# Experts whose first 128 slots take only batches 0 to 2, in a retention-plus-experts kernel

## The chip, the cores and the metric

The kernel runs on one core of a Trainium2 chip. The engines are named as the profile names them: PE (TensorE, matrix products), DVE (VectorE), ACT (ScalarE), POOL (GpSimd), SP (SyncE); DMA queues are fed by SP, ACT and POOL. The metric is the device time of one execution in microseconds, as the median of several runs. Before the change it is 261.54 us (three runs, 259.69 to 262.08). The profiled execution took 259.74 us, and its trace spans 257.9 us of that; times inside the kernel are counted from the start of that span.

## What is computed

Two stages follow each other. The first is a retention layer (4 batches, 8 heads, 768 tokens, head size 64). Its output rows are the input of the second, a mixture of 8 experts of which each row takes one, or none.

```python
def _attn_ref(q, k, v):                       # state decays by gamma of the head
    for t in range(S):
        state = gamma * state + einsum('bhd,bhe->bhde', k[:, :, t], v[:, :, t])
        y[:, :, t] = scale * einsum('bhd,bhde->bhe', q[:, :, t], state)

def _moe_ref(x, w_skip, w_gate, w1, w2):      # x: 3072 rows of 512
    do_compute = x @ w_skip > 0
    out = x.copy()                            # rows that are skipped stay as they are
    xc = x[do_compute]
    e_idx = argmax(xc @ w_gate)               # 8 experts, one for each row
    gate_w = softmax(xc @ w_gate)[e_idx]
    for e in range(8):
        h = maximum(xc[mask] @ w1[e], 0)      # 512 -> 1024
        y[mask] = gate_w[mask] * (h @ w2[e])  # 1024 -> 512
    out[do_compute] = xc + y
```

In the given input 1510 of the 3072 rows are computed. Counted from the reference's own input, an expert gets 133 to 229 rows of all four batches, and 98 to 164 rows of batches 0 to 2.

## The kernel before

The retention stage goes through 16 units (4 batches, 4 pairs of heads each). A unit's result is spread over two iterations: iteration `i` makes the masked products of unit `i` and adds up unit `i-1`.

```python
    for i in range(NU):                       # NU = 16
        scale_qk(i + 1)                       # POOL: decay factors into k and q
        if i == 0:
            more_constants()                  # POOL iotas, DVE casts
        if i in wunits:
            load_w(*wjobs.pop(0), poolW)      # weights of experts 0 to 3, POOL queue
        load(i + 3)
        for g in range(G):
            t_qk(i, kw, KT, "KT", 1, g)       # PE transposes, ACT copies
            t_qk(i, qw, QT, "QT", 2, g)
        s_at(i, 0)                            # PE products, DVE mask (ATm)
        if i >= 2:
            t_x(i - 2, 0); t_x(i - 2, 1)      # PE transposes to rows, ACT copies, rows to DRAM
        if i >= 1:
            s_inter(i - 1)                    # PE into Y (two PSUM tiles)
        # ... steps of the routing of an earlier batch ...
        s_at(i, 1); s_kv(i); s_av(i - 1, 0); s_at(i, 2); s_av(i - 1, 1)
```

`s_av` ends with two copies out of PSUM that free `Y`:

```python
        xT[i] = pool.tile([128, NS, 128], FP32, tag="xT", bufs=5, name="xT")
        for c in range(2):
            (V_.tensor_copy if c == 1 and i == NU - 1 else A_.copy)(out=xT[i]..., in_=Y[i, c]...)
```

Routing gives each computed row a slot of its expert: 256 slots an expert (`CAP`), in two halves of 128 (`NST = 2`). A row's place is a running count over the rows before it (`places`, `put_places`); one-hot matrices and a matmul (`one_hots`, `slot_table`) turn places into a table `T` of slot to row (`slot_rows` gives the indices `si`) and slot to gate weight (`slot_gates` gives `g`). For batches 0 to 2 this is done inside the loop. For batch 3 it comes after the last unit, in a row:

```python
    L = gate_rows(range(NP - 1))
    s_av(z, 0); s_av(z, 1)
    gate_last(z, L)
    t_x(z, 0); t_x(z, 1)                      # the last rows of `out` leave
    Ls, ha = route(L)
    cp = places(B - 1, ha)
    put_rhs(B - 1, ha, IDS)
    put_places(B - 1, ha, cp)
    oh = one_hots(pool, B - 1)
    slot_table(psum, B - 1, oh, IDS, "T", 4)
    si = slot_rows()
    gate_weight(B - 1, Ls, ha)
    put_rhs(B - 1, ha, GTS)
    slot_table(psum, B - 1, oh, GTS, "T", 4)
    g = slot_gates()
```

Only then come the experts. Rows are fetched from `out` by slot with an indirect DMA, put through the two layers, and written back with an indirect DMA. The weights of experts 4 to 7 are loaded in this stage (`late`: eight loads of 1 MB as bf16), since they take the space of the retention stage.

```python
    for e in range(3):
        gather(e, si, first=True)             # two halves of 128 rows
        load_w(*late.pop(0))
    x_tr(0)                                   # DVE cast, PE transposes, DVE copy
    for e in range(E):
        hT = layer1(e)                        # 32 matmuls, N = 256; ACT relu
        if e + 1 < E:
            x_tr(e + 1)
        layer2(e, hT, si, g, first=True)      # 16 matmuls, N = 512; DVE gate and add; scatter
        with tc.issue_after(scatters[-1].ins):
            if e + 3 < E:
                gather(e + 3, si, first=True)
            for _ in range(2):
                if late:
                    load_w(*late.pop(0))
```

After the experts the kernel reads how many rows the fullest expert has, and repeats the stage for slots above 256 if there are any. Here there are none.

Of the kernel before, what the change touches and what calls it, by code (L numbers as in the profile page):

```python
# [18 lines left out]
def kernel(  # L19
# [24 lines left out]
    R = 3  # L44
# [11 lines left out]
    NEARLY = 4  # L56
    scale = 1.0 / math.sqrt(D)
    lng = [math.log(1.0 - 2.0 ** (-5.0 - h)) for h in range(H)]

    poolC = ctx.enter_context(tc.tile_pool(name="constp", bufs=1))  # L60
    poolW = ctx.enter_context(tc.tile_pool(name="wpool", bufs=1))

# [3 lines left out]
    psum = st1.enter_context(tc.tile_pool(name="rps", bufs=1, space=bass.MemoryType.PSUM))  # L66
    stM = ExitStack()
    ET = mybir.EngineType
    stM.enter_context(tc.manual_schedule(engines={ET.PE, ET.DVE, ET.Activation, ET.Pool, ET.SP}))
# [69 lines left out]
    NV = 6  # L139
# [17 lines left out]
    def clear_table():  # L157
        V_.memset(T[:, :, :, :], 0.0)
        V_.memset(T[:, :, 0, :], float(N // (128 * R)))

    def more_constants():
# [7 lines left out]
        chv_i = poolC.tile([128, NCHT], I32, name="chv_i")  # L169
        G_.iota(chv_i[:, :], pattern=[[1, NCHT // R], [0, R]], base=-(N // (128 * R)), channel_multiplier=0)  # L170
        row_i = poolC.tile([128, 1], I32, name="row_i")
        G_.iota(row_i[:, :], pattern=[[0, 1]], base=0, channel_multiplier=1)
        r_i = poolC.tile([128, NCHT], I32, name="r_i")
        G_.iota(r_i[:, :], pattern=[[0, NCHT // R], [1, R]], base=0, channel_multiplier=0)
# [10 lines left out]
        V_.tensor_copy(vals[:, :, 0], chv_i[:, :])  # L185
        V_.tensor_copy(vals[:, :, 1], row_i[:, :].to_broadcast([128, NCHT]))
        V_.tensor_copy(vals[:, :, 2], r_i[:, :])
# [7 lines left out]
    def load_w(e, which, pl):  # L195
        if which == 0:
            w1b[e] = pl.tile([128, NDB, F], BF16, tag=f"w1_{e}", bufs=1, name="w1b")
            G_.dma_start(out=w1b[e][:, :, :], in_=moe_w1[e].rearrange("(p a) f -> p a f", p=128))
        else:
            w2b[e] = pl.tile([128, NFB, DM], BF16, tag=f"w2_{e}", bufs=1, name="w2b")  # L200
            G_.dma_start(out=w2b[e][:, :, :].rearrange("p (j r) d -> p j (r d)", r=2), in_=moe_w2[e].rearrange("(j p r) d -> p j (r d)", p=128, r=2))
# [73 lines left out]
    def s_av(i, g):  # L275
# [11 lines left out]
        xT[i] = pool.tile([128, NS, 128], FP32, tag="xT", bufs=5, name="xT")  # L287
        for c in range(2):
            (V_.tensor_copy if c == 1 and i == NU - 1 else A_.copy)(  # L289
                out=xT[i][:, :, 64 * c : 64 * c + 64], in_=Y[i, c][:, :, :].rearrange("p g (r t) -> p (g r) t", r=R)  # L290
            )

    def t_x(i, a):
# [5 lines left out]
        if last and a == 0:  # L299
            xall["last"] = pool.tile([128, NS, 128], FP32, tag="xlast", bufs=1, name="xlast")  # L300
# [15 lines left out]
        else:  # L316
            cs = slice(DM - 128, DM) if last else slice(0, DM - 128)
            src = xall["last"][:, :, :] if last else xall[b][:, :, cs]
            for g in range(G):
                A_.dma_start(  # L320
                    out=rows[g * 128 * R : (g + 1) * 128 * R, cs].rearrange("(p r) d -> p r d", r=R),
                    in_=src[:, g * R : (g + 1) * R, :],
                )

# [13 lines left out]
    def gate_rows(pairs, halves=(0, 1), L=None):  # L338

        n = len(pairs)  # L340
        if L is None:
            L = pool.tile([128, NS, E + 1], FP32, tag="L", bufs=2, name="L")
# [17 lines left out]
    def st(name, shape, dt=FP32):  # L360
        return pool.tile(shape, dt, tag=name, bufs=1, name=name)
# [42 lines left out]

    def put_rhs(b, ha, ns):
# [7 lines left out]
    def gate_weight(b, Ls, ha):  # L413
# [4 lines left out]
        rs = st("rs", [128, E])  # L418
        V_.tensor_reduce(out=rs[:, :], in_=ha[:, :, :].rearrange("p c e -> p e c"), axis=AXX, op=ALU.add)  # L419
        V_.tensor_tensor(Rsum[:, :], Rsum[:, :], rs[:, :], ALU.add)  # L420
# [5 lines left out]
        gp = vals[:, js, :]  # L426
        V_.tensor_copy(gp[:, :, 3], gw[:, :])
        V_.tensor_tensor(gw[:, :], gw[:, :], gp[:, :, 3], ALU.subtract)
        V_.tensor_copy(gp[:, :, 4], gw[:, :])
        V_.tensor_tensor(gp[:, :, 5], gw[:, :], gp[:, :, 4], ALU.subtract)  # L430

    def one_hots(pl, b):
        oh = []
        for j in range(b * NS, (b + 1) * NS):
            o = pl.tile([128, CAP], BF16, tag="oh", bufs=NS, name="oh")
            V_.tensor_scalar(o[:, :], iotab[:, :], posT[:, j : j + 1], None, ALU.is_equal)
            oh.append(o)
        return oh

    def slot_table(ps, b, oh, ns, tag, bufs):  # L440

        tp = ps.tile([128, NST, ns.stop - ns.start, E], FP32, tag=tag, bufs=bufs, name="tabps")
        for s_ in range(NST):
# [5 lines left out]
        V_.tensor_tensor(T[:, :, ns, :], T[:, :, ns, :], tp[:, :, :, :], ALU.add)  # L449


    ALLV, IDS, GTS = slice(0, NV), slice(0, 3), slice(3, NV)
    wjobs = [(e, w) for e in range(NEARLY) for w in range(2)]
    wunits = (1, 3, 5, 7, 9, 11, 13, 14)
    routed = oh = None
    for i in range(NU):
        scale_qk(i + 1)
        if i == 0:
# [5 lines left out]
        for g in range(G):  # L464
            t_qk(i, kw, KT, "KT", 1, g)
            t_qk(i, qw, QT, "QT", 2, g)
        s_at(i, 0)
        if i >= 2:
# [4 lines left out]
        if i >= 6 and p == 3:  # L473
            slot_table(psum, b - 1, oh, ALLV, "T", 4)
        if i >= 2 and p == 3:
            gate_logits(b, range(NP))
        if i >= 6 and p == 0:
            L = gate_rows(range(NP))
        if i >= 6 and p == 1:
            cp = places(b - 1, routed[1])  # L480
        s_at(i, 1)
        s_kv(i)
        if i >= 1:
            s_av(i - 1, 0)
        s_at(i, 2)
        if i >= 1:
# [4 lines left out]
        if i >= 6 and p == 0:  # L491
            routed = route(L)
        if i >= 6 and p == 1:
            put_places(b - 1, routed[1], cp)
            oh = one_hots(pool, b - 1)
        if i >= 6 and p == 2:
# [5 lines left out]
    gate_weight(B - 2, *routed)  # L502
    put_rhs(B - 2, routed[1], ALLV)
# [4 lines left out]
    slot_table(psum, B - 2, oh, ALLV, "T", 4)  # L508
    L = gate_rows(range(NP - 1))
    s_av(z, 0)  # L510
# [4 lines left out]
    Ls, ha = route(L)  # L515
    cp = places(B - 1, ha)
    put_rhs(B - 1, ha, IDS)
    put_places(B - 1, ha, cp)
    oh = one_hots(pool, B - 1)
    slot_table(psum, B - 1, oh, IDS, "T", 4)  # L520

    def slot_rows():

        sh = [128, NST, E]
        sf = poolC.tile(sh, FP32, tag="sf", bufs=1, name="sf")
        V_.scalar_tensor_tensor(out=sf[:, :, :], in0=T[:, :, 1, :], scalar=float(R), in1=T[:, :, 2, :], op0=ALU.mult, op1=ALU.add)
        si = poolC.tile(sh, I32, tag="si", bufs=1, name="si")
        V_.scalar_tensor_tensor(
            out=si[:, :, :], in0=T[:, :, 0, :], scalar=float(128 * R), in1=sf[:, :, :], op0=ALU.mult, op1=ALU.add
        )  # L530
        return si

    def slot_gates():
        g = poolC.tile([128, NST, E], FP32, tag="g", bufs=1, name="g")
        V_.tensor_tensor(g[:, :, :], T[:, :, 3, :], T[:, :, 4, :], ALU.add)
        V_.tensor_tensor(g[:, :, :], g[:, :, :], T[:, :, 5, :], ALU.add)
        return g

    si = slot_rows()
    gate_weight(B - 1, Ls, ha)  # L540
    put_rhs(B - 1, ha, GTS)
    slot_table(psum, B - 1, oh, GTS, "T", 4)
    g = slot_gates()
    st1.close()


    poolX = ctx.enter_context(tc.tile_pool(name="wlate", bufs=1, reuse_waits="tile"))
    poolE = ctx.enter_context(tc.tile_pool(name="esb", bufs=2, reuse_waits="tile"))
    psE = ctx.enter_context(tc.tile_pool(name="eps", bufs=2, space=bass.MemoryType.PSUM, reuse_waits="tile"))
# [140 lines left out]
```

## Time and profile before

| Stage | from, us | to, us | what ends it |
|---|---|---|---|
| first loads and constants | 0 | 6.7 | first PE transposes |
| retention, 16 units | 6.7 | 160.1 | last matmul of `s_av(15)` |
| routing of batch 3, first gathers | 160.1 | 173.9 | first matmul of layer 1 |
| eight experts | 173.9 | 245.9 | last matmul of layer 2 |
| last scatters, count, end | 245.9 | 257.9 | end of the span |

PE is busy 215.5 us of the span (84%), DVE 134.2, POOL 95.5, ACT 77.5. The table is read as follows: where PE is busy nearly all the time, its work sets the length of the stage; where it is not, something that PE waits for does. A line `line engine op out<-in` of the profile names the source line, the engine, and the tiles; in the list of waits, `A <- B: t, n, m` says that engine and tile A waited for B for t us in all, n times, the longest m us.

### The profile page before, as it was taken

The numbers are of one execution on the slowest core, as the hardware profiler recorded it, in microseconds if no ns is written. First come the engines' busy times: TensorE is split into PE (matmuls) and PEld (weight loads), VectorE is DVE, ScalarE is ACT, GpSimd is POOL, SyncE is SP. The second block draws the span as 40 slices with busy tenths as digits, with TensorE's granted clock in tenths as the row PEclk, the third lists the DMA queues.
The fourth block names the chain that finished last, engine by engine and source line by source line (L and its number), as shares of the span: only waits on it lengthen the run. The fifth ranks groups of instructions, "written<-read, shape, count | busy, mean of one in ns | idle before, by whom it ended". The sixth has DMA issues, their size and how long they took to land. (4 is left out here: it accounts for less than half of the span.)

```text
span 257.9 us, 7338 instructions
## 1 busy us (share of the span) xinstructions
PE 215.5 (84%) x3121; PEld 169.9 (66%) x3129; DVE 134.2 (52%) x402; ACT 77.5 (30%) x174; POOL 95.5 (37%) x100
## 2 busy tenths in 40 slices
PE   0689999999999999999999988529999395999910
PEld 0468788868987878888778876427666254566600
DVE  3676566635757764766864674672453142334210
ACT  2202553263145335314524513103222303023300
POOL 6635252434244333343423000084475264252230
PEclk9979999999999999999999999756999979799995
DMA  6977949779989499799398604269999999631120
GB/s 200 333 204 187 267 137 206 211 201 230 347 212 243 130 226 315 221 245 260 79 187 256 121 4 158 89 140 220 257 217 220 253 215 269 202 99 59 51 79 0
DMA packets 36788, 48.67 MB, mean 189 GB/s; under 512 B 3236, under 2 KB 29348, under 8 KB 35728
## 3 DMA queue, kind: packets, MB, share of 16 engines
q0 software_dynamic: 7936, 22.97, 42.1%
q1 hardware_dynamic: 26400, 18.90, 24.4%
q10 hardware_dynamic: 2416, 6.29, 6.2%
q8 instruction: 26, 0.43, 0.7%
q14 instruction: 10, 0.08, 0.1%
HBM read 56.64 MB, written 10.49 MB: 260 GB/s over the span
## 5 line engine op out<-in xcount | busy, mean ns | idle before, releaser
L235 DVE TENSOR_TENSOR ATm<-atps,maskc 128x384 f32<-128x384 f32 x96 | 49.0, 552 | 43.4 <-PE atps L230 42.9
L230 PE MATMUL atps<-QT,KT 64*64 64x192 f32 x768 | 44.7, 342 | 6.8 <-ACT QT L217 3.9
L95 POOL TENSOR_TENSOR ks<-kw,tk 128x768 f32<-128x768 f32 x16 | 23.9, 1492 | 44.9 <-PE kvps L251 42.4
L230 PEld LDWEIGHTS atps<-QT,KT 64*64 64x64 f32 x768 | 28.5, 136 | 16.2 <-ACT QT L217 7.5
L281 PE MATMUL yps<-ATm,vn 64*64 64x192 f32 x768 | 38.9, 325 | 0.0
L590 ACT ACTIVATE hT<-hps 128x512 bf16<-128x512 f32 x32 | 19.1, 597 | 59.1 <-PE hps L586 59.1
L95 POOL TENSOR_TENSOR qs<-qw,tq 128x768 f32<-128x768 f32 x15 | 22.7, 1516 | 35.2 <-issue 34.0
L289 ACT COPY xT<-yps 128x384 f32<-128x384 f32 x31 | 13.4, 482 | 71.4 <-PE yps L281 71.4
L586 PE MATMUL hps<-xgT,w1b 128*128 128x256 bf16 x256 | 31.6, 285 | 0.5 <-DVE xgT L578 0.5
L597 PE MATMUL yps<-w2b,hT 128*128 128x512 bf16 x120 | 31.1, 405 | 0.6 <-issue 0.2
L281 PEld LDWEIGHTS yps<-ATm,vn 64*64 64x64 f32 x768 | 30.4, 133 | 0.3 <-issue 0.2
L586 PEld LDWEIGHTS <-w1b 128*128 128x128 bf16 x256 | 26.3, 103 | 6.1 <-issue 0.7
L557 POOL DMA_INDIRECT xg<-out_dram,si x16 | 16.9, 1055 | 34.9 <-DVE rs L419 28.7
L605 POOL DMA_INDIRECT out_dram<-yo,si x16 | 16.6, 1039 | 35.1 <-DVE yo L602 30.1
L602 DVE SCALAR_TENSOR_TENSOR yo<-yps,g,xg 128x512 f32<-128x512 f32 x16 | 12.0, 751 | 23.6 <-PE yps L597 23.6
L597 PEld LDWEIGHTS <-hT 128*128 128x128 bf16 x128 | 13.0, 104 | 15.3 <-issue 3.7
L216 PE MATMUL tps<-ident,ks 128*128 128x128 f32 x96 | 17.3, 291 | 6.7 <-POOL ks L95 6.7
L217 ACT COPY KT<-tps 128x384 f32<-128x384 f32 x32 | 16.1, 505 | 14.2 <-PE tps L216 14.2
L270 PE MATMUL yps<-QT,Zb 128*128 128x192 f32 x96 | 18.5, 328 | 1.0 <-ACT xT L289 1.0
L216 PEld LDWEIGHTS tps<-ident,ks 128*128 128x128 f32 x96 | 11.2, 145 | 11.0 <-POOL ks L95 6.7
L571 DVE CAST xb<-xg 128x512 bf16<-128x512 f32 x16 | 9.6, 638 | 16.1 <-DMA xg<-out_dram,si 16.0
L217 ACT COPY QT<-tps 128x384 f32<-128x384 f32 x32 | 16.5, 516 | 0.5 <-PE tps L216 0.5
(107 smaller groups left out, 241.5 us busy)
## 6 DMA issues: line engine op xcount, KB each, us to landing
w1b<-in_moe_w_dram POOLq DMA_DIRECT2D x8, 1024.0 KB, 11.6
w2b<-in_moe_w_dram POOLq DMA_DIRECT2D x8, 1024.0 KB, 10.4
kw<-in_k_dram SPq DMA_DIRECT2D x16, 384.0 KB, 5.7
qw<-in_q_dram SPq DMA_DIRECT2D x16, 384.0 KB, 4.8
vn<-in_v_dram SPq DMA_DIRECT2D x16, 384.0 KB, 5.4
out_dram<-xall ACTq DMA_DIRECT2D x3, 1536.0 KB, 13.3
out_dram<-xall ACTq DMA_DIRECT2D x2, 576.0 KB, 3.8
out_dram<-xlast ACTq DMA_DIRECT2D x2, 192.0 KB, 2.4
```

The lines of the kernel that those rows point to most:

```text
L95: eng.tensor_tensor(o[:, :, :, :], in_, sc, ALU.mult)
L216: PE.transpose(out=ps[:, j * 128 : (j + 1) * 128], in_=in_, identity=ident[:, :])
L217: A_.copy(out=dst[i][:, g * R : (g + 1) * R, :], in_=ps[:, :].rearrange("p (j t) -> p j t", j=R))
L230: PE.matmul(out=ps[h][cp, j * C : (j + 1) * C], lhsT=KT[i][hp, s_, cp], rhs=QT[i][hp, R * g : R * g + R, cp], start=True, stop=True,)
L235: V_.tensor_tensor(out=ATm[i, n][:, h, :, :], in0=ps[h][:, :].rearrange("p (c t) -> p c t", c=2), in1=maskc[:, 2 * n : 2 * n + 2, :, :].re ...
L270: PE.matmul(out=Y[i, c][:, g, :], lhsT=Zb[i % 2][ch - 1][:, :], rhs=QT[i][:, R * g : R * g + R, 64 * c : 64 * c + 64], start=(ch <= 2), st ...
L281: PE.matmul(out=Y[i, c][64 * h : 64 * h + 64, g, :], lhsT=vn[i][cp, h * G + g, r * D : (r + 1) * D], rhs=ATm[i, s_ // 2][cp, h, s_ % 2, :] ...
L557: ga = G_.indirect_dma_start(out=t[:, :], out_offset=None, in_=out[:, :], in_offset=bass.IndirectOffsetOnAxis(ap=si[:, st, e : e + 1], axi ...
L586: PE.matmul(out=ps[:, f, :], lhsT=w1b[e][:, db, f2 * 256 + f : (f2 + 1) * 256 : 2], rhs=xgT[e][:, db, :], start=(db == 0), stop=(db == NDB ...
L590: A_.activation(out=hT[:, 2 * f2 : 2 * f2 + 2, :], in_=ps[:, :, :], func=AF.Relu, bias=0.0, scale=1.0)
L597: PE.matmul(out=ps[:, :], lhsT=hT[:, fb, st * 128 : (st + 1) * 128], rhs=w2b[e][:, fb, :], start=(fb == 0), stop=(fb == NFB - 1),)
L605: sc = G_.indirect_dma_start(out=out[:, :], out_offset=bass.IndirectOffsetOnAxis(ap=si[:, st, e : e + 1], axis=0), in_=yo[:, :], in_offset ...
```

## The change

The first half of each expert's slots (0 to 127) takes rows of batches 0 to 2 only. After batch 2 the count of each expert is raised to 128 where it is lower (`pad_counts`), so that a row of batch 3 always goes to slot 128 or later. The first half is then known before batch 3 is routed, and its rows can be fetched and computed while batch 3 is being finished. For three experts (`NSPLIT`) the two halves become separate tasks: first the first halves of experts 0 to 2, then their second halves, then experts 3 to 7 whole.

The routing of batch 3 (places, table, gate weights) is spread over the first two tasks. The first three gathers are issued in the last unit of the loop, and read from the rows of batches 0 to 2 alone. The loads of weights of experts 4 to 7 begin once the last rows of batch 3 have reached DRAM, one a task.

Other parts go with it. Of the two copies out of `Y` the second goes to DVE in every unit. `more_constants` moves from unit 0 to unit 1. The slot table holds a row number in two parts (16s and rest) in place of three, which makes 5 values a row and not 6. The routing steps of a batch come earlier in the units. PSUM is one pool for the whole kernel, so the experts use the tiles of the retention stage (two for layer 1 in place of three). The stores of batch 3's rows go on SP's queue in place of ACT's.

```diff
-        if i == 0:
+        if i == 1:
             more_constants()
@@ s_av
-            (V_.tensor_copy if c == 1 and i == NU - 1 else A_.copy)(
+            (A_.copy if c == 0 else V_.tensor_copy)(
@@ t_x, batch 3
-                A_.dma_start(
+                last_out = nc.sync.dma_start(
@@ new
+    def pad_counts():
+        cnt = psum.tile([128, E], FP32, tag="T", bufs=4, name="cnt")
+        PE.matmul(out=cnt[:, :], lhsT=onesb[:, :], rhs=Rsum[:, :], start=True, stop=True)
+        pad = poolS.tile([128, E], FP32, tag="pad", bufs=1, name="pad")
+        V_.tensor_scalar(pad[:, :], cnt[:, :], -1.0, 128.0, ALU.mult, ALU.add)
+        V_.tensor_scalar(pad[:, :], pad[:, :], 0.0, ident[:, 0:1], ALU.max, ALU.mult)
+        V_.tensor_tensor(Rsum[:, :], Rsum[:, :], pad[:, :], ALU.add)
@@ gather
+        n = (B - 1) * S if first and s_ == 0 else N      # the first half reads batches 0 to 2
@@ the loop over units
+        if i == NU - 1:
+            tp = table(B - 2, oh, ALLV)
+            pad_counts()
         s_at(i, 2)
+        if i == NU - 1:
+            add_table(tp)
+            slot_values(0)                               # si[0], gt[0]
+            for e in range(NSPLIT):
+                gather(e, 0)
         if i >= 1:
             s_av(i - 1, 1)
@@ after the loop
     s_inter(z)
     t_x(z - 1, 0)
     gate_logits(B - 1, range(NP - 1))
     t_x(z - 1, 1)
+    x_cast(0, 0)
     L = gate_rows(range(NP - 1))
+    x_tr(0, [0])
+    x_cast(1, 0)
     s_av(z, 0)
...
+    tasks = [(e, [0]) for e in range(NSPLIT)] + [(e, [1]) for e in range(NSPLIT)] + [(e, [0, 1]) for e in range(NSPLIT, E)]
+    for t, (e, sts) in enumerate(tasks):
+        hT = layer1(e, sts)                              # N = 128 for a half
+        if t == 0:
+            cp = places(B - 1, ha); put_places(B - 1, ha, cp)
+            oh = one_hots(B - 1, 1); put_rhs(B - 1, ha, IDS)
+        # x_cast and x_tr of the next task
+        yps = [layer2(e, s_, hT, n) for n, s_ in enumerate(sts)] if len(sts) == 1 else None
+        if t == 0:
+            # table of batch 3's rows, second half: si[1]
+        if t == 1:
+            # count, gate_weight, put_rhs, table of batch 3's gate weights: gt[1]
+        if t == 0:
+            ld = load_w(*late.pop(0))                    # waits for the last rows
+            gather(0, 1)
+        put_out(...)                                     # gate and add, scatter
+        if t == 0:
+            for n in range(1, NSPLIT): gather(n, 1)
+        nxt = {1: 3, 3: 4, 4: 5, 5: 6, 6: 7}.get(t)
+        if nxt is not None:
+            for s_ in range(NST): gather(nxt, s_)
+        if late:
+            load_w(*late.pop(0))
```

## The prediction

> **What bounds the kernel now.** I read the slices first, then busy time by stage, then the timeline of the places where PE stands still, then the waits. The chain of work that ended last holds only the last scatter (two pieces, 1.16 us) and tells nothing about the stages before it.
>
> ```profile
> PE   0689999999999999999999988529999395999910
> PEclk9979999999999999999999999756999979799995
> DMA  6977949779989499799398604269999999631120
> ```
>
> PE is at 90% or more from 20 us to about 155 us, so the retention stage is PE's own work. There are three holes: the start, 160 to 174 us, and near 204 us. The granted clock falls after each. DMA is full from 175 to 220 us.
>
> ```profile
> core 0: us, PE busy (x) PEld busy (x) DVE busy (x) ACT busy (x) POOL busy (x), PEclk, DMA share, GB/s
> 143.90:152.60 8.70, 8.44 (x166) 7.43 (x163) 5.34 (x19) 3.25 (x8) 0.00 (x0) 1.00 0.23 44
> 160.10:173.90 13.80, 5.59 (x62) 4.34 (x59) 9.53 (x42) 1.58 (x4) 5.58 (x6) 0.68 0.51 131
> 173.90:202.10 28.20, 27.98 (x197) 19.67 (x199) 10.38 (x18) 8.97 (x16) 14.94 (x16) 0.92 1.04 228
> 206.30:245.90 39.60, 36.32 (x235) 22.91 (x240) 13.62 (x24) 9.55 (x16) 16.29 (x16) 0.92 0.56 146
> 245.90:257.90 12.00, 0.00 (x0) 0.00 (x0) 0.75 (x1) 0.00 (x0) 1.29 (x2) 0.69 0.12 42
> ```
>
> From 160.1 to 173.9 us PE does 5.6 us of work. The timeline of PE shows why:
>
> ```profile
> 160.93 1.48 PE L357 MATMUL lps<-Wc,xT 128*128 128x9 f32 x12 [0.80 <-DVE xT L289]
> 169.44 0.50 PE L445 MATMUL tabps<-rhsT,oh 128*128 128x24 bf16 x12 [3.04 <-DVE rhsT L409]
> 171.56 0.61 PE L577 MATMUL xtp<-identb,xb 128*128 128x128 bf16 x4 [1.61 <-DVE xb L571]
> 173.92 5.96 PE L586 MATMUL hps<-xgT,w1b 128*128 128x256 bf16 x32 [0.51 <-DVE xgT L578]
> 191.00 3.66 PE L586 MATMUL hps<-xgT,w1b 128*128 128x256 bf16 x32
> 194.94 3.62 PE L597 MATMUL yps<-w2b,hT 128*128 128x512 bf16 x15
> ```
>
> Route, places, table, indices, gather, cast and transposes follow one another, each waiting for the one before. The first layer 1 then takes 5.96 us at the lower clock, against 3.66 later. An undisturbed expert repeats every 7.39 us (third at 190.79, fourth at 198.18). Eight without gaps would be 58.6 us (8 x 7.39, less 0.5 for a next transpose that the last lacks); from 173.9 to 245.9 there are 72.0. So 13.4 us go to waits and low clock.
>
> ```profile
> DVE xb L571 <- DMA xg<-out_dram,si: 16.0, 5, 6.2
> POOL out_dram L605 <- DMA w1b<-in_moe_w_dram: 4.3, 1, 4.3
> PEld atps L230 <- ACT QT L217: 7.5, 15, 0.6
> PE atps L230 <- DVE ATm L235: 2.9, 1, 2.9
> ```
>
> The first line is the later holes: rows that arrive behind weight loads. The third is a short wait in every unit, as ACT copies two `xT` tiles before it gets to `KT` and `QT`. The last is at 11 to 14 us, where DVE stands at `more_constants`.
>
> [...] 5.96 against 3.66 us for the same 32 matmuls, and the clock was 0.50 from 165 to 174 us. [...] Here eight such transposes take 0.50 us until layer 2 follows (186.99 to 187.49 us), 62.5 ns each; I take that. [...]
>
> **Part 1: the hole after the retention stage.** The three first gathers leave in unit 15, so layer 1 needs nothing from batch 3. I follow the end of unit 15 on the clock of the trace before.
> - DVE gains work in unit 15: places and one-hots 1.67 us and count 0.4 before the second mask, then pad 0.55, table add 0.25, three slot operations 0.5, and only then the `xT` copy (0.56), which frees half of `Y`. I get that copy's end at 155.4 us, where both copies ended at 153.5 before. `s_inter(15)` needs it, so PE waits some 1.8 us longer.
> - Indices at 154.5 and a first gather of 3.3 us (as the first one before) give rows at 158.0 and a cast at 158.6; PE reaches that transpose at 159.3. No wait.
> - `s_av(15)` ends at 161.9, copies at 162.5, the last gate matmuls at 163.8, the last `t_x` at 164.6. Layer 1 starts there, not at 173.9: 9.3 us earlier, with PE warm.
>
> **Part 2: the experts.** A half task is 32 matmuls of N=128 (2.0 us), four transposes (0.25) and half of layer 2 (1.65): 3.9 us. Two halves are 7.8 against 7.39, so splitting three experts costs 1.2 us, and 0.25 more for the last one's wider transpose. The batch 3 routing adds 0.9 us of PE (places 0.4, two tables of 0.25). The gate weights are a chain on DVE after the second task's row cast (count 0.4, eight small operations of about 0.2, `rhsT` 0.3); PE reaches their table some 1.2 us too soon. So: 6 x 3.9 + 0.25 + 0.9 + 1.2 = 25.8 us for the half tasks, then 5 x 7.39 - 0.5 = 36.5, in all 62.3 us without a DMA wait. From 164.6 that ends at 226.9, against 245.9: 19.0 us less.
>
> **Part 3: do the weights keep up?** Before, the loads from 170.4 us on, with 21 gathers and scatters between them, ended near 222 us. From landings I take 5.3 us a load and 0.44 an indirect transfer (8 x 5.3 + 21 x 0.44 = 51.6). Now the first load waits for the last rows (about 167.7), and the second is issued after three POOL instructions of 1.4 us that follow the first scatter, near 175; 1.5 to 2 us of DMA are lost there. From then loads are issued faster than they land. The rows of experts 4 to 7 land at about 193, 199, 205 and 212 and the last weights near 217 to 219; PE asks for rows at 194, 201, 209, 216 and for the last weights at 224. That is 1 to 7 us to spare. POOL's waits before fit a limit of eight transfers in flight on its queue (the scatter that waited 4.3 us is the eighth after that load; so is the gather that waited 2.0), and the same limit holds some issues back now. I add 1.5 us for a stall.
>
> **Part 4: the loop and the start.** ACT drops one of two copies (0.43 us) ahead of `KT`, so the wait of `s_at` on `QT` (0.25 us of PE in most units) mostly goes: 14 x 0.2 = 2.8 us less. DVE takes 16 x 0.56 us more; at 12 of 20 us it has room. `more_constants` in unit 1 removes the 2.9 us wait in unit 0, but POOL's constants now stand behind `ks` and `qs` of unit 2, and these wait for unit 0 and 1. I get DVE free at 21.3 us and PE's next products at 21.9, where they began at 21.98 before. So the wait moves and nothing is gained; a colder clock may cost 1 us. Net for this part: about 2 us less.
>
> **Part 5: nothing elsewhere.** The last 12 us stay. With padding the fullest expert has 229 rows, under 256, so no further pass. The stores' move from ACT's queue to SP's is off PE's path.
>
> **Sum.** -19.0 (parts 1 and 2) +1.5 (part 3) -2 (part 4) = -19.5 us. I found few waits beside those that I looked for, and such sums lean to the good side, so I take -18: 261.5 - 18 = 243.5 us.
>
> **Rivals.** (a) DMA becomes the bound. The bytes are the same, DMA was full from 175 to 220 us, and the loads start only about 2 us sooner. For it: my slack is 1 to 7 us, and one stall over 2.6 us brings the low clock back (the one before 218 us made layer 2 take 5.30 us, not 3.62). Against it: the half tasks need no late weights for 26 us. If it holds, the end follows the last weights by one expert: about 250 to 253 us. (b) DVE becomes the bound in unit 15 and the first two tasks: route, places, one-hots, casts and gate weights in one queue. The trace has such a cast at 1.39 us in place of 0.43. Each microsecond of it is on PE's path: 246 to 249 us. (c) N=128 gains nothing over N=256, if weight loads set the pace: six half tasks would each be 1.6 us longer, nearly 10 us, so 253 us. Against it: the 62.5 ns of the transposes. (d) The loop loses from DVE's copies and the earlier routing steps: up to 3 us.
>
> **Range and chances.** Rivals (a) and (b) in part make 247 to 251; if part 4 and the slack are better than I think, 238. So 238 to 250. To miss a 2% gain (256.3 us) three quarters of the hole would have to return as another wait; I give that 4%, and slower 1%.
>
> **What would show it.** The first layer 1 matmul at 161 to 166 us, at full clock; N=128 layer 1 near 2.0 us; a stall of about 1 us at the gate-weight table; no wait of a row cast on DMA over 2 us; the wait of `QT` reduced; unit 2 starting no earlier than 26 us; the end 12 us after the last layer 2. The prediction is wrong if PE stands still for late rows or weights after 190 us, or if the half tasks take 5 us each.

## The result and the profile after

The changed kernel takes 250.13 us (median of four executions, 246.94 to 250.44), the kernel before 260.75 on the same chip: a ratio of 0.956, with a 95% interval of 0.947 to 0.966. That is faster by over 2%, and 6.6 us above the predicted 243.5, at the upper end of the range of 238 to 250. The trace spans 248.4 us, where it was 257.9. The ratios here and below leave out executions at a visibly lower granted clock, which the medians include; of the experiments "count late", "fetch late" and "count and rows" the profiled execution was such a one, so that only lengths at full clock and the kind of wait are read from it.

Again the slices first: PE's busy tenths, the granted clock, and the DMA engines' share, in 40 slices of 6.2 us.

```profile
PE   0897999999998999997999999789689949999910
PEclk9998999999999999999999999999999988999985
DMA  6998739959978949989847990274999999995120
```

The wide hole after the retention stage is gone and the clock stays up through it. Two small dents are left in the expert stage, near 180 us and 200 us, and only the second is followed by a lower clock (0.62 from 202.5 to 206.0 us; 1.00 from 181.3 to 184.0). DMA is full from about 174 to 223 us. The 7 at 155 to 161 us is in unit 15.

The stages (columns as in the table before: stretch, its length, busy time and instructions of each engine, clock, DMA share, GB/s). The first two are an ordinary unit and unit 7, then the former hole, then the tail.

```profile
44.19:52.44 8.25, 8.23 (x161) 7.15 (x157) 5.74 (x16) 2.97 (x7) 2.99 (x2) 1.00 0.83 214
70.93:81.72 10.79, 9.57 (x167) 7.60 (x163) 10.26 (x31) 3.11 (x8) 3.73 (x3) 1.00 0.81 179
164.60:167.42 2.82, 2.02 (x19) 2.04 (x19) 1.11 (x6) 0.60 (x2) 0.00 (x0) 1.00 0.51 188
237.13:248.40 11.27, 0.01 (x1) 0.00 (x0) 1.38 (x5) 0.00 (x0) 1.30 (x2) 0.67 0.12 44
```

From the last `s_av` to the first layer 1 are 2.82 us, where there were 13.8. Unit 7 takes 10.79 us, where it took 8.65; DVE is nearly full in it.

The timeline of PE (start, duration, operation, idle time before it in brackets):

```profile
165.40 1.48 PE L364 MATMUL lps<-Wc,xT 128*128 128x9 f32 x12 [0.80 <-DVE thr L694]
167.42 1.95 PE L607 MATMUL hps<-xgT,w1b 128*128 128x128 bf16 x32
176.62 0.31 PE L456 MATMUL tabps<-rhsT,oh 128*128 128x24 bf16 x6 [0.86 <-DVE rhsT L422]
181.26 0.40 PE L512 MATMUL xtp<-identb,xb 128*128 128x128 bf16 x4 [2.53 <-DVE xb L503]
201.61 0.40 PE L512 MATMUL xtp<-identb,xb 128*128 128x128 bf16 x4 [3.17 <-DVE xb L503]
202.57 5.30 PE L617 MATMUL yps<-w2b,hT 128*128 128x512 bf16 x16
207.71 3.69 PE L607 MATMUL hps<-xgT,w1b 128*128 128x256 bf16 x32
```

The first layer 1 runs at full clock (1.00 from 167.42 to 169.37 us). The wait of 2.53 us is for the second half's first rows, the one of 3.17 us (0.33 follow) for the rows of expert 4. After the second, layer 2 begins at 202.57 and the next layer 1 only at 207.71, 5.14 us later; in the following expert it is 3.46 (211.68 to 215.14), so the low clock took 1.7 us more. PE had asked for these rows at 198.4 us, the end of the layer 1 before. In the table of waits (engine and line, what it waited for, total us, times, longest):

```profile
DVE xb L503 <- DMA xg<-out_dram,si: 10.7, 3, 5.2
PEld atps L232 <- ACT QT L219: 2.0, 8, 0.3
```

The row cast that PE waits for both times waits itself for gathered rows. The wait for `QT` went from 7.5 to 2.0 us.

Where the 9.5 us of span came from: units 0 and 1 end 1.6 us later (unit 2 at 27.68, it was 26.11), units 2 to 14 take 2.0 us more, unit 15 to its last `s_av` 0.9 more (17.14, it was 16.24), the hole 11.0 less, the experts (first layer 1 to last layer 2) 2.3 less (69.71, they were 71.97), the tail 0.7 less.

### The profile page after: what moved, and what is told of

Read it like the earlier page. It is cut to its first block, busy times and chain, and to the rows that moved or that the text cites. A ratio compares the mean times of both kernels' runs of the same rounds, so it can differ in the third digit from the quotient of the medians.

```text
span 248.4 us, 7552 instructions
## 1 busy us (share of the span) xinstructions
PE 215.5 (87%) x3214; PEld 170.7 (69%) x3214; DVE 143.4 (58%) x424; ACT 72.8 (29%) x159; POOL 95.6 (38%) x98
## 4 chain that ended last, share of the span: by engine, by line
PE 58%; DVE 16%; issue 11%; POOL 6%; DMA 4%; ACT 1%; POOLq 0%; DVEq 0%; ACTq 0%
PE atps L232 13%; PE yps L283 8%; PE yps L617 8%; PE tps L218 7%; PE hps L607 6%; DVE ATm L237 5%; PE yps L272 5%; DMA xg<-out_dram,si 4%; PE tps L307 4%; PE kvps L253 3%; POOL xg L493 2%; PE gps L338 2%; DVE oh L447 2%; DVE Zb L265 1%; DVE Rsum L416 1%
## 5 line engine op out<-in xcount | busy, mean ns | idle before, releaser
L232 PE MATMUL atps<-QT,KT 64*64 64x192 f32 x768 | 48.0, 344 | 5.4 <-DVE ATm L237 4.6
L232 PEld LDWEIGHTS atps<-QT,KT 64*64 64x64 f32 x768 | 29.7, 137 | 16.9 <-DVE ATm L237 8.3
L283 PE MATMUL yps<-ATm,vn 64*64 64x192 f32 x768 | 40.7, 331 | 0.0
L283 PEld LDWEIGHTS yps<-ATm,vn 64*64 64x64 f32 x768 | 31.9, 136 | 0.4
L291 ACT COPY xT<-yps 128x384 f32<-128x384 f32 x16 | 7.7, 479 | 78.0 <-PE yps L283 78.0
L607 PE MATMUL hps<-xgT,w1b 128*128 128x128 bf16 (+1 forms) x352 | 30.1, 243 | 0.0
L628 POOL DMA_INDIRECT out_dram<-yo,si x16 | 17.3, 1080 | 20.5 <-DVE yo L625 17.7
L625 DVE SCALAR_TENSOR_TENSOR yo<-yps,gt,xg 128x512 f32<-128x512 f32 x16 | 12.0, 750 | 21.3 <-PE yps L617 20.2
L617 PEld LDWEIGHTS <-hT 128*128 128x128 bf16 x128 | 12.5, 101 | 13.8 <-issue 2.3
L309 ACT COPY xall<-tps 128x384 f32<-128x384 f32 x30 | 13.0, 482 | 15.8 <-PE tps L307 15.8
L253 PEld LDWEIGHTS kvps<-vn,ks 64*64 64x64 f32 x576 | 16.7, 145 | 0.4
```

What stands on the lines that cost most here:

```text
L232: PE.matmul(out=ps[h][cp, j * C : (j + 1) * C], lhsT=KT[i][hp, s_, cp], rhs=QT[i][hp, R * g : R * g + R, cp], start=True, stop=True,)
L253: PE.matmul(out=ps[c][64 * h : 64 * h + 64, g * D : (g + 1) * D], lhsT=kw[i][cp, R * g + r, h, :], rhs=vn[i][cp, h * G + g, r * D : (r + 1 ...
L283: PE.matmul(out=Y[i, c][64 * h : 64 * h + 64, g, :], lhsT=vn[i][cp, h * G + g, r * D : (r + 1) * D], rhs=ATm[i, s_ // 2][cp, h, s_ % 2, :] ...
L607: PE.matmul(out=ps[:, f, :], lhsT=w1b[e][:, db, f2 * 256 + fr : (f2 + 1) * 256 : 2], rhs=xgT[e][:, db, 0:n], start=(db == 0), stop=(db == ...
L617: PE.matmul(out=ps[:, :], lhsT=hT[:, fb, n * 128 : (n + 1) * 128], rhs=w2b[e][:, fb, :], start=(fb == 0), stop=(fb == NFB - 1),)
L628: sc = G_.indirect_dma_start(out=out[:, :], out_offset=bass.IndirectOffsetOnAxis(ap=si[s_][:, e : e + 1], axis=0), in_=yo[:, :], in_offset ...
```

## The experiments

Each kernel is the changed one with the edit shown. The ratio is to the kernel before, on the same chip in the same session.

| kernel | median us | ratio, 95% interval | first layer 1 at | experts us |
|---|---|---|---|---|
| changed kernel | 250.13 | 0.956, 0.947 to 0.966 | 167.42 | 69.71 |
| count late | 247.34 | 0.943, 0.936 to 0.951 | 166.57 | 69.70 |
| constants in unit 0 | 251.01 | 0.957, 0.949 to 0.965 | 167.32 | 71.32 |
| one late load | 247.62 | 0.947, 0.939 to 0.954 | 166.09 | 68.61 |
| ACT copies both | 252.57 | none | 166.45 | 72.20 |
| rows first | 245.19 | 0.948, 0.940 to 0.956 | 165.29 | 65.60 |
| no row wait | 251.19 | 0.967, 0.961 to 0.974 | 165.62 | 73.76 |
| fetch late | 253.78 | 0.971, 0.958 to 0.983 | 169.42 | 71.54 |
| count and rows | 245.22 | 0.935, 0.927 to 0.943 | 164.50 | 69.99 |
| all three | 242.89 | 0.932, 0.923 to 0.941 | 163.44 | 66.26 |
| early pair | 251.58 | 0.972, 0.964 to 0.980 | 164.62 | 71.58 |
| no weights | 239.81 | 0.921, 0.912 to 0.931 | 167.02 | 61.83 |

Against the changed kernel's own interval, only "count and rows", "all three" and "no weights" lie clear below. For the others the lengths in the trace, of one execution each, are the evidence, and not the whole time.

The theory from this profile: units 7 and 11 lose to DVE operations that moved ahead of a mask, and the experts lose to rows that land behind weight loads. Rivals: DMA bandwidth itself, or the engines' own time in the half tasks.

### Count late

Unit 7 on DVE first, then POOL and PE, in the changed kernel:

```profile
76.12 1.26 DVE L447 TENSOR_SCALAR oh<-iotab,posT 128x256 bf16<-128x256 bf16 x6
77.30 0.23 DVE L415 TENSOR_REDUCE rs<-ha 128x8 f32<-128x48 bf16 x1
77.56 1.39 DVE L416 TENSOR_TENSOR Rsum<-Rsum,rs 128x8 bf16<-128x8 bf16 x1
78.88 1.01 DVE L237 TENSOR_TENSOR ATm<-atps,maskc 128x384 f32<-128x384 f32 x2
77.44 1.49 POOL L99 TENSOR_TENSOR ks<-kw,tk 128x768 f32<-128x768 f32 x1 [2.60 <-PE kvps L253]
79.48 1.18 PE L232 MATMUL atps<-QT,KT 64*64 64x192 f32 x13 [1.15 <-DVE ATm L237]
```

An addition of 8 columns takes 1.39 us and ends with POOL's product (77.44 + 1.49 = 78.93). The mask `ATm` stands behind it, and PE behind the mask for 1.15 us. The edit moves the count to the end of those units:

```diff
-            count(routed[1])                     # ahead of the second mask
+            if i == NU - 1:
+                count(routed[1])
@@ end of the unit
+        if i >= 6 and p == 1 and i < NU - 1:
+            count(routed[1])
```

> Units 7 and 11 of the changed kernel take 10.79 us each, others 8.25. Theory: the count (two small DVE operations after the one-hots) is stopped there by POOL's multiply, 1.39 us in place of 0.17, and the second mask product of the unit waits behind it. With the count at the end of these two units they should take 8.3 to 8.6 us, the last unit start some 4.4 us earlier (near 143.1 us), and the whole take about 246 us, if the experts' waits for rows stay as they are. Rival: the one-hots themselves (1.27 us) hold DVE up, or POOL stops the next small operation instead. Then the units stay above 9.5 us and the time near 248 to 250.

Measured: units 7 and 11 at 9.22 and 9.21 us in place of 10.79, and 247.34 us. DVE in unit 7 of this kernel:

```profile
76.33 1.01 DVE L237 TENSOR_TENSOR ATm<-atps,maskc 128x384 f32<-128x384 f32 x2
80.43 0.17 DVE L416 TENSOR_TENSOR Rsum<-Rsum,rs 128x8 bf16<-128x8 bf16 x1
```

Away from POOL's product the same addition takes 0.17 us. Not every DVE operation is stretched: two masks, which read `atps` in PSUM and `maskc` in SBUF, took 1.01 us beside the same product here (76.47 to 77.96 us), as much as away from it (1.02 us at 78.77), while the addition in the changed kernel, with `Rsum` and `rs` both in SBUF, stood 1.39 us. What sets the two apart, no run tests. Some 1.6 of the 2.1 us a unit had lost are thus the count; the one-hots, still ahead of the mask, are a part of the rest (0.3 us, see "all three").

The loop as a whole did not get shorter by that: unit 15 starts at 146.62 us (147.46 in the changed kernel, 143.1 expected). Unit 8 took 12.12 us, where it took 8.59; PE stood 2.04 us in it with no releaser shown, and the clock was lower after it: 16 matmuls of `s_at` took 1.56 us from 83.04 us and 0.88 us from 87.19. Unit 8 is longer in all five kernels that move the count (9.64 to 12.41 us; 8.45 to 8.59 in the other seven), but unit 12, behind the second moved count, is not (8.45 us here). What stops PE there stays open.

### Constants in unit 0

```diff
-        if i == 1:
+        if i == 0:
             more_constants()
```

> The constants are made in unit 0 again. Theory: the move only shifted a wait of DVE on POOL's constants from unit 0 to unit 1, and made it dearer, since PE's clock falls again. Unit 2 then starts at about 26.1 us, as in the kernel before, and not at 27.68, and the time is some 1.6 us less, about 248.5. Rival: the move helped, as it was meant to (unit 1 starts at 16.10 with it and at 18.44 without), and something else takes the 3.9 us of units 1 and 2; then unit 2 starts later than 27.7 and the time is 252 or more.

Measured: PE waits 3.54 us in unit 0 and unit 2 starts at 27.04 us. With the constants in unit 1 it starts between 25.9 and 27.8 in ten kernels whose first two units are the same (24.4 with ACT's copies, below). The move gains nothing that stands out of that spread, as Part 4 said.

### One late load

Experts 4 to 7 compute with the weights of experts 0 to 3, apart from one matrix that is still fetched; seven loads and their 14 MB are left out, so the output differs.

```diff
-    late = [(e, w, poolX) for e in range(NEARLY, E) for w in range(2)]
+    late = [(e, w, poolX) for e in range(NEARLY, NEARLY + 1) for w in range(1)]
+    w2b[NEARLY] = w2b[0]
+    for e in range(NEARLY + 1, E):
+        w1b[e], w2b[e] = w1b[e - NEARLY], w2b[e - NEARLY]
```

> Leaves out seven of the eight late weight loads: experts 5 to 7 use the weights of experts 1 to 3, and expert 4 has a first layer of its own but the second layer of expert 0. All products and transfers of rows stay. Theory: the waits of the experts are rows that stand behind weight loads in POOL's queue: 2.5 us at 178.7, 3.2 at 198.4, and about 1.7 us of a slower PE clock after the second. Without the loads both go (perhaps a rest at the first, as one load is left), so the experts take 62 to 65 us from first to last product and not 69.7, and the whole 243 to 245 us. Rival: the waits come from the order of the tasks on DVE and POOL (a row fetch is issued only after a scatter of the task before); then at least one wait of 2 us stays and the time is 247 or more.

Measured: 247.62 us and experts of 68.61. A wait of 2.47 us near 180 us stays, for which the trace names no releaser; the one load left still stands ahead of the second half's rows. The wait for expert 4's rows is gone, but PE stood for 0.63 and 1.81 us on `hT` from 192 to 195 us and at a clock of 0.69 after it, a stop of which the trace shows no cause. So this run showed only that the second wait needs the loads; the last experiment asks again.

### ACT copies both

```diff
-            (A_.copy if c == 0 else V_.tensor_copy)(
+            (V_.tensor_copy if c == 1 and i == NU - 1 else A_.copy)(
```

> Both copies out of Y go to ACT again, as in the kernel before (the last unit aside). Theory: ordinary units go from 8.25 back to 8.48 us, some 3 us in 14 units, and the wait of 1.73 us before the last unit's products with the state falls to about 1, so the time is about 252 us. Rival: the copies on DVE are what costs the loop time (DVE is 9 us busier); then units 7 and 11 come down from 10.79 and the time is 247 to 249.

Measured: ordinary units at 8.48 us again (8.25 in the changed kernel), units 7 and 11 at 11.46, and the wait for `QT` is back in part:

```profile
PEld atps L232 <- ACT QT L219: 3.7, 10, 0.5
```

The DVE copy brings the predicted 0.2 us in an ordinary unit, and it is not what lengthens units 7 and 11. Over the whole loop it brings nothing that shows: unit 15 starts at 146.40 us here, and at 145.33 to 147.46 in the five kernels with the loop of the changed one, because unit 2 started at 24.42 us and not at 25.9 to 27.8. DVE's copies may thus be what the start lost; no further run asks. The median, 252.57 us, has no interval; the lengths alone are the evidence.

### Rows first

POOL's issues in the changed kernel, the weight loads and the first gather of expert 4 (other gathers and scatters between them left out):

```profile
171.43 0.59 POOL L200 DMA_DIRECT2D w1b<-in_moe_w_dram  x1 [10.08 <-issue]
177.68 0.82 POOL L203 DMA_DIRECT2D w2b<-in_moe_w_dram  x1
182.63 0.61 POOL L200 DMA_DIRECT2D w1b<-in_moe_w_dram  x1
185.64 0.80 POOL L203 DMA_DIRECT2D w2b<-in_moe_w_dram  x1
189.66 1.04 POOL L493 DMA_INDIRECT xg<-out_dram,si  x1 [0.30 <-issue]
```

Four loads stand ahead of these rows, which land at 200.9 us. In the traces of both original kernels each transfer of POOL's queue landed after the one issued before it: here the four loads at 180.4, 187.3, 194.0 and 199.6 us, and the rows 11.3 us after their issue. In the kernel before gathers landed 3.3 us after their issue at best, 7.7 at the median and 11.8 at worst. The edit issues no load in the third task, so that three stand ahead and each later load comes one task later:

```diff
-            if late:
+            if late and t != 2:
                 load_w(*late.pop(0))
```

> The third task issues no weight load; each later load moves on by one task, so the rows of expert 4 stand behind three loads and not four, and those of experts 5 to 7 likewise behind one fewer. Theory: the experts' waits are one account, the arrival of expert 4's rows behind all that was put in the queue before them (in four kernels so far the two waits differed, 2.53 and 3.17, 1.53 and 4.72, 2.50 and 2.89, 0.30 and 5.97 us, but their sum was 5.4 to 6.3). With one load less ahead, some 5.3 us, the rows land near 195 us, the second wait goes, and with it the slower clock after it (1.7 us): experts 65 us in place of 69.7, the whole about 245.5. The first wait, 2.5 us near 179, stays. Rival: the queue is full anyway, so the same wait comes at expert 5, or at the last weights, and the experts stay at 69 us or more.

Measured: 245.19 us; experts 65.60 us, 4.1 less. PE:

```profile
178.95 0.40 PE L512 MATMUL xtp<-identb,xb 128*128 128x128 bf16 x4 [2.35 <-DVE xb L503]
227.26 3.63 PE L617 MATMUL yps<-w2b,hT 128*128 128x512 bf16 x16 [0.98 <-DMA w2b<-in_moe_w_dram]
```

No wait lies between these two: the rows of expert 4 come in time. In their place the last weights are late by 0.98 us. The bytes are the same, so the 3.5 us and the 1.7 us of lower clock were the order in the queue, not the bandwidth; the last weights come next.

### No row wait

The first late load no longer waits until the last rows have reached DRAM.

```diff
             ld = load_w(*late.pop(0))
-            tc.add_manual_dep(ld.ins, last_outs[-1].ins.name, ...)   # "the rows leave first"
```

> The first late load no longer waits for the last rows to reach DRAM. In the changed kernel it is issued at 171.4 us, 4 us after the first product of the experts. Theory: everything in the queue behind it comes earlier by as much as it does. If it goes out at 166 us, both waits (2.5 and 3.2 us) shrink to under 1 in sum, experts near 64 us, the whole about 244. Rival 1: the load shares the transfer engines with the last rows' stores, which land some us later, and the fetch of second halves waits for them: the first wait grows to 4 us or more and nothing is gained. Rival 2: its buffer lies where the retention stage has its own, so it waits for the same stores anyway, and the times do not move.

Measured: no gain, 251.19 us. The load is issued at 163.16 us, 8.3 us sooner, but the first gather of the second half at 173.39 (172.43 in the changed kernel) and the second load at 178.66 (177.68). The wait for the second half's rows fell to 0.16 us, and that for expert 4's grew to 6.01.

### Fetch late

In the program, the three first gathers and casts come after the loop in place of inside unit 15 and right behind it.

```diff
-            for e in range(NSPLIT):              # in unit 15
-                gather(e, 0)
@@ after the last s_av
+    for e in range(NSPLIT):
+        gather(e, 0)
+    x_cast(0, 0)
+    x_tr(0, [0])
+    x_cast(1, 0)
```

> Undoes the early fetch alone: the three first gathers are issued after the last unit's rows are done, and the first two casts and the first transposes come after batch 3's routing on DVE. Tasks, split and weights stay. Theory: the early fetch is what closes the hole. Gathers then leave near 166 us, rows land 3.3 us later, and cast, transposes and copy take 1.7 more: the first product of the experts comes at about 171.5 and not 167.4, on a PE whose clock has fallen, so 4 to 6 us are lost at the start. As the weights are issued at the same time as now, part of it comes out of the later waits: the whole 251 to 254 us. Rival: the start of the experts is worth nothing as long as expert 4's rows set the time; then the second wait shrinks by what the start loses, and the whole stays at 250 within 1 us.

Measured: 253.78 us. But the gathers did not leave later. POOL issues nothing between the two places, so the first was issued at 157.23 us (157.63 in the changed kernel), and not near 166 as expected:

```profile
157.23 1.08 POOL L493 DMA_INDIRECT xg<-out_dram,si  x1 [15.60 <-DVE gt L472]
```

Only the casts and transposes moved, behind batch 3's routing on DVE. Between the last `s_av` and layer 1 are 5.4 us in place of 2.8, with a wait of 0.68 us for the cast and 0.52 for its copy, and the first layer 1 then takes 3.57 us at a lower clock (1.95 in the changed kernel). So 2.6 us of the hole are the place of the casts and transposes. What the early gathers are worth, no run shows. That they and the routing off the path make up the other 8.4 of the 11.0 us is read from the two traces (before, these steps stood in a row from 160.1 to 173.9 us), not tested by a run.

### Count and rows

Both edits, "count late" and "rows first".

> Both gains that have stood so far, in one kernel: the second bookkeeping of batches 0 and 1 (row sums, running counts) at the end of units 7 and 11, and no weight load between the rows of expert 2 and those of expert 4. If they are two separate costs, they add: units 7 and 11 at 9.2 us (10.8 in the changed kernel), the experts from first layer 1 to last layer 2 at 65.6 us as with the rows first alone, and about 242 us (245.2 less 3). Rival: the weights arrive by the DMA's clock and not by the first expert's start, so an earlier start of layer 1 by 1.5 to 3 us only lengthens the wait for the last weights (0.98 us with the rows first alone) to 2.5 to 4 us, and the time stays at 244 to 245 us.

Measured: a ratio of 0.935, against 0.948 for the rows alone (the intervals touch at 0.940 to 0.943). 0.935 of 259.48 is 242.6 us, what the sum of the two single gains would give, but as the intervals touch, that they add is not shown. Units 7 and 11 took 9.2 us. The profile also shows the rival's wait, 2.25 us for the last weights, so part of an earlier start is lost there.

### All three

"Count and rows", and two more edits:

```diff
-        if i >= 6 and p == 1:
+        if i >= 6 and p == 1 and i == NU - 1:
             # places, one-hots ahead of the second mask
@@ after the second mask
+        if i >= 6 and p == 1 and i < NU - 1:
+            put_places(b - 1, routed[1], cp)
+            oh = one_hots(b - 1)
@@ s_av
-            (A_.copy if c == 0 else V_.tensor_copy)(
+            (A_.copy if c == 0 or i == NU - 2 else V_.tensor_copy)(
```

> As the run with the count and the rows, and two more: in units 7 and 11 the places and one-hots are made after the second mask, so that nothing stands ahead of it on VectorE, and ScalarE takes the copy of the second xT half of unit 14, so that VectorE reaches the masks of unit 15 sooner. Theory: units 7 and 11 fall from 9.2 to 8.4 to 8.8 us, the wait of PE ahead of the last s_inter from 1.7 to about 1.0 us, and the time is about 1.5 to 2 us under the run with the count and the rows, 240 to 241 us. Rival: POOL gathers the rows of those units later because their places are written later, and the experts wait for their last weights for as long as layer 1 starts earlier: the same time as the run with the count and the rows.

Measured: 242.89 us, a ratio of 0.932 (0.923 to 0.941): not to be told from "count and rows" by the time, but under both original kernels. Units 7 and 11 fell to 8.95 (8.4 to 8.8 expected), and the wait ahead of the last `s_inter` from 1.73 to 0.95 us, as expected. But units that get the moved work rose: units 11 and 12 together take 18.27 us, against 17.67 with the count alone moved. Units 7 to 12 take 55.35 us, against 55.32 in "count and rows", so that step gained nothing. Of the 0.8 us that the copy took off the wait, 0.3 show in the length of unit 15 (16.87, it was 17.14). The experts, 66.26 us, hold a first layer 1 of 3.41 us at a clock of 0.54, where "rows first" has 1.95.

### Early pair

"All three", and both matrices of expert 4 are issued ahead of the second half's rows, without waiting for the last rows to leave.

```diff
-            ld = load_w(*late.pop(0))
-            tc.add_manual_dep(ld.ins, last_outs[-1].ins.name, ...)
+            load_w(*late.pop(0))
+            load_w(*late.pop(0))
             gather(0, 1)
@@ the end of a task
-            if late and t != 2:
+            if late and t not in (0, 2):
                 load_w(*late.pop(0))
```

> As the run with all three, with both matrices of expert 4 fetched without waiting until the rows of experts 0 to 3 have left, ahead of the gathers of the second half's rows; so two weight loads move from the busy stretch after 177 us into the stretch at 163 to 175 us, where the DMA engines were busy for a third of the time. Theory: the wait for the last weights disappears and the experts take 63 to 64.5 us, 1 to 2 us under the run with all three. Rival: two loads of 2 MB stand ahead of the second half's rows in POOL's queue, so that layer 1 of that half waits 4 us or more in place of 2.4, and the time is that of the run with all three or 1 to 3 us above it.

Measured: the rival, and more, 251.58 us. The store of the last rows (`xlast`, SP's queue; the last column is the median us from issue to landing) from 155 to 180 us, first in "all three":

```profile
out_dram<-xlast SPq DMA_DIRECT2D x2, 192.0 KB, 2.4
```

The same line in "no row wait":

```profile
out_dram<-xlast SPq DMA_DIRECT2D x2, 192.0 KB, 5.9
```

And in "early pair":

```profile
out_dram<-xlast SPq DMA_DIRECT2D x2, 192.0 KB, 10.4
```

With no, one and two loads ahead it lands after 2.4, 5.9 and 10.4 us. The second half's rows are read from what it writes, so in "early pair" their first gather was issued at 177.49 us (169.95 in "all three"), and PE waited 3.90 us. The wait for the rows, which leaves the DMA engines at a share of 0.64 from 163 to 175 us in "all three" (not a third, as expected), protects the path.

### No weights

"All three", and experts 4 to 7 use the matrices of experts 0 to 3; all eight late loads are left out, so the output differs.

```diff
-    late = [(e, w, poolX) for e in range(NEARLY, E) for w in range(2)]
+    for e in range(NEARLY, E):
+        w1b[e], w2b[e] = w1b[e - NEARLY], w2b[e - NEARLY]
+    late = []
```

> As the run with all three, and no weights are fetched during the experts at all: experts 4 to 7 are computed with the matrices of experts 0 to 3, so the output differs and 16 MB are not read. It asks whether the sum of Part 2 (62.3 us from first layer 1 to last layer 2) is the engines' own time. Theory, that the late weights and the rows behind them are what lengthened the experts: 62.3 to 63.5 us here, PE waiting less than 1 us for rows after the gate-weight table, and 237.5 to 239.5 us in all. Rival, that something else in the experts lengthens them (gathers and scatters of rows, ScalarE and VectorE evictions between PE and PE): 65 us or more, with waits of PE on hT or xb of 1 us or more, and the time at that of the run with all three, 241 to 243 us.

Measured: experts of 61.83 us, 239.81 us in all. The time is above the expected one because PE stood 1.80 us in unit 8, again without a releaser, and the loop ended late. The experts up to the first whole one and from there on, first in "rows first", then here (columns as above):

```profile
165.29:192.88 27.59, 24.15 (x289) 17.28 (x287) 15.16 (x48) 7.82 (x15) 16.43 (x17) 1.00 0.87 201
192.88:230.89 38.01, 37.03 (x274) 25.14 (x272) 15.47 (x26) 11.95 (x20) 18.69 (x20) 1.00 0.93 220
```

```profile
167.02:192.01 24.99, 23.98 (x289) 17.38 (x287) 15.08 (x48) 8.03 (x15) 14.08 (x13) 1.00 0.33 102
192.01:228.85 36.84, 36.84 (x274) 25.25 (x272) 14.84 (x26) 11.94 (x20) 15.50 (x16) 1.00 0.24 80
```

With DMA a quarter to a third busy, PE is busy for all of the second stretch. The only wait of PE left in the experts is 0.86 us at the gate-weight table.

## Why the prediction was right and wrong, point by point

**Part 1, right.** Route, rows and casts left the path: 2.82 us from `s_av` to layer 1, where 2.7 were worked out (161.9 to 164.6), at full clock. The full clock was luck in part: of the twelve kernels measured with the change, six took 3.0 to 3.6 us for this first layer 1 and six took 1.95. Layer 1 began at 167.42 us, outside the 161 to 166 of the prediction, since the loop ended 2.7 us late. PE's wait for the later `xT` copy in unit 15 is 1.73 us, where there were 0.95; 1.8 longer was predicted. Rival (b) is left with those 0.8 us: after unit 15, PE waits for DVE in the batch 3 routing only 0.86 us, at the gate-weight table (1.2 predicted). How much of the gain is the early fetch alone, no run parts.

**Part 2, right.** Layer 1 at N=128 takes 1.95 us (2.0), 61 ns a matmul, which ends rival (c). "No weights" measures the sum by itself: 61.83 us against 62.3; to the first whole expert 25.0 (25.8), then 36.8 (36.5).

**Part 3, wrong, and the larger miss.** The step that failed is "1 to 7 us to spare" for the rows, with a stall of 1.5 us. The prediction called itself wrong if PE stood still for late rows after 190 us, and PE did, for 3.17 us from 198.4 us. In the changed kernel the late weights cost 7.9 us (69.71 - 61.83). Of these, 2.5 are the wait for the second half's rows, 3.5 that for expert 4's and 1.7 the clock after it. Two terms were off. The first late load left at 171.4 us and not at 167.7 (2.7 of these 3.7 us are the loop's late end, `s_av` at 164.6 and not 161.9), and the second half's rows, which I did not count among those that stand behind a load, were next in the queue. And the rows of expert 4 landed at 200.9 us and not 193, with four loads ahead; PE asked for them at 198.4 and not 194. "Rows first" takes one of the four away and the second wait goes; "no weights" takes all and the first goes too. Rival (a) named the time, 250 to 253 us, but not the reason: in the changed kernel the last weights, issued at 214.2 us, landed 13.6 us later, and layer 2 used them at 233.5. The wait is one of order, up to the last weights, which bind next (0.98 us).

**Part 4, wrong in sign.** Units 2 to 13 without 7 and 11 take 2.9 us less, for the predicted 2.8, but that agreement is luck in part: in "ACT copies both" these ten units take 1.6 us more, which is the copy's share, and the other 1.3 us, mostly in units 9 and 13, came with the rest of the change. The step "DVE takes 16 x 0.56 us more; at 12 of 20 us it has room" judged DVE by its mean. In units 7 and 11 it has none: the moved one-hots and count stand ahead of the mask, and the count's addition takes 1.39 us beside POOL's product (0.17 away from it). That is +2.1 us in each. The trace before had the sign: rival (b) names a cast of 1.39 us in place of 0.43, which lies beside a POOL product (89.42 to 90.92 us), but the prediction looks for it in unit 15 and the first two tasks only. Unit 14 took 0.6 more; with ACT's copies it took 8.96 us in place of 9.73, so DVE's copies are part of that. So units 2 to 14 took +2.0 in place of -2.8; this is rival (d). The start cost 1.6 us where some 0.8 was allowed, within the spread of unit 2's start (25.9 to 27.8 us).

**Part 5, right.** The tail is 11.3 us (12.0).

**Sum.** The parts gave -19.5; the spans give -9.5. Of the 10.0 us between, 4.8 are the loop, 5.9 the experts (69.71 less 62.3 and 1.5), 0.8 the start and 0.1 the hole; unit 15 and the tail give 1.6 back. The rounding to -18 covered 1.5 of it.

## What to carry to other kernels

Room on an engine is counted at the instruction that another engine waits for, in the unit that gets the moved work, and not by its mean over the loop. When small gathers and large loads share a queue, list for each gather the loads that stand ahead of it, and move one load behind it before anything else is tried; here one moved line gave 4 us in the experts. Where an edit moves an issue in the program, read its time in the trace before the result: in "fetch late" the gathers stayed where they were. A transfer that seems to idle behind a wait may be keeping the DMA engines free for the store that the path needs: here it landed after 2.4 us, and after 10.4 with two loads issued ahead of it.

## What the runs showed of the hardware that I had not expected

- The 192 KB row stores landed after 2.4 us alone, and 5.9 and 10.4 us with one and two weight loads issued ahead on another queue: a separate queue did not keep them apart.
- A DVE addition of 128x8 took 0.17 us alone and 1.39 us beside a POOL product; a cast of 128x6, with one input, took 0.18 and 1.36 us (both in unit 7 of the changed kernel).
- After waits of 2.35 ("rows first") and 2.53 us PE's clock stayed at full (half a layer 2 of 1.89 us); after one of 2.65 and 0.19 us (kernel before) and one of 3.17 and 0.33 us it was lower (a layer 2 of 5.30 us both times, in place of 3.62). But in "all three" the clock was 0.54 from 163.4 to 167.0 us, and the first layer 1 took 3.41 us, after idle times of less than 1 us, and in "count late" and "no weights" 16 matmuls of `s_at` took 1.56 us in place of 0.88 after waits of 2.04 and 1.80 us. The first layer 1 was slow (3.01 to 3.57 us) also in "constants in unit 0", "ACT copies both", "fetch late", "count and rows" and "early pair"; no run explains it.
- In three of the five kernels that move the count, PE stood 1.4 to 2.0 us in unit 8, twice without a releaser. The DMA engines were busy then (9 and 8 tenths in the slices from 74 to 87 us of "count late"), and the page of that run lists 27 packets of instruction transfers (0.44 MB) among their work over the whole span; whether PE waited for instructions, no run tests.
